# The Fourier transform of an attention block in plain float32: column tiles, a second feature fold, and a new written order

## The chip, the cores and the metric

The kernel runs on one core of a Trainium2 chip. The metric is device time in microseconds (us) of one launch, median of several runs. Engines are named as in the profile: PE (TensorE matmul), PEld (its weight loads), DVE (VectorE), ACT (ScalarE), POOL (GpSimd), SP (SyncE, which issues most DMAs).

## The reference

Softcapped attention over 4 batches, 12 heads, 448 tokens, head size 64; then a real two-dimensional Fourier transform over tokens and features, a layer norm and a feed-forward block:

```python
scores = cap * np.tanh(scale * (q @ k.T) / cap)
x = softmax(scores) @ v                # heads side by side: (4, 448, 768)
u = x + np.real(fft(fft(x, axis=1), axis=2))
un = (u - mean(u)) / sqrt(var(u) + 1e-6)
out = u + relu(un @ w_ch1) @ w_ch2     # 768 -> 3072 -> 768
```

The weights come as float64 values and are converted on the chip.

## The kernel before, in words

Nearly every large matmul is made of three float32r products: an operand is split into a head (a cast to float32r) and a rest (value minus head), and rest times head, head times rest and head times head are summed in PSUM. The weighing of v by the attention weights is the exception: it is in plain float32, and its 114 query rows are written as two column tiles of the array, output partitions 0 to 63 and 64 to 113.

*Attention.* Twelve heads of a batch make six pairs. Each pair has seven units of 128 keys; two units at a time go through `scores` (PE, line 428), `tanh` and `exp` (ACT, lines 438 and 441) and `weigh` (PE, line 459). `denominators` and `normalise` (DVE) write the batch's `u`.

*Transform of one batch.* A real transform needs only sums and differences of mirrored tokens and features. The queries are gathered so that the 448 tokens lie in four groups: odd, even, and the mirrors of both. `fold_tokens` adds and subtracts mirrored tokens; `fold_features` does so for a feature d and d + 384, so that 384 features are left, in three pieces of 128. There are two sorts, `sd` 0 and 1, for even and odd feature frequencies. `fold_split` and `fold_rest` split the result. `stage1` (line 527) is the transform over tokens: per piece and sort 12 matmuls of 226 columns with the constants `seqT`. `split_y` and `rest_y` split its result out of PSUM. `stage2` (line 551) is the transform over features: for cosine and sine (`n`) and odd and even tokens (`par`), 18 matmuls of 192 or 194 columns with the constants `featT`, themselves split by `constant`. `add_u`, `moments`, `rows`, `standardise`, `u_cols` and `u_copy` add it to u, standardise, and turn u around.

*Feed-forward.* `up` (line 761) and `down` (line 790) walk 12 groups of two blocks of 128 hidden features, over four batches, 36 matmuls of 448 columns each time; `first`, `second` and `third` convert the weights beside them on DVE and ACT.

*Order.* Each engine runs its instructions in program order. That order is written out: the table `ORDER` gives each call a place (`at`), calls are sorted by place and issued. From the second group of the feed-forward on, a fixed pattern takes over. Buffers are named by tag and count in `new`; PSUM results of `stage1`, `stage2`, `u_cols`, `rows_cols` and half of `down` share the tag `d` with two buffers, and scores have two buffers of their own.

Of the kernel before, what the change touches and what calls it, by code (L numbers as in the profile page):

```python
# [11 lines left out]
F32 = mybir.dt.float32  # L12
# [21 lines left out]
ODD = list(range(1, S // 2, 2))  # L34
EVEN = [0, S // 2] + list(range(2, S // 2, 2))
# [15 lines left out]
NJE, NJO = DM // 4 + 2, DM // 4  # L51
NJ = NJE + NJO
# [25 lines left out]
    [("y", 6)] * 6,  # L78
    [("qkr", 3)] * 3 + ["x1"] * 3,
    [("feat", 6)] * 6,  # L80
)
XCPLACE = [[(f"xc{b}", 3)] * 3 for b in range(3)] + [[("f", 2), ("f", 2), ("t", 1)]]
# [5 lines left out]
        313, 314, 296, 298, 539, 541, 592, 593, 786, 789, 794, 795, 987, 994, 988, 993  # L88
    ],
    "constant": [  # L90
        87, 36, 217, 35, 172, 14, 288, 12
    ],
    "denominators": [
        60, 84, 114, 153, 190, 227, 266, 323, 353, 397, 422, 469, 526, 560, 598, 634, 665, 714, 774, 814, 841,
        884, 920, 950
    ],
    "exp": [
# [4 lines left out]
    ],  # L102
    "fetch": [
        9, 62, 140, 155, 193, 203, 306, 307, 514, 636, 996, 1013, 1016, 1059
    ],
    "fold_features": [
        127, 92, 201, 169, 239, 255, 352, 368, 409, 421, 485, 488, 585, 588, 667, 649, 726, 722, 824, 822, 911,
        903, 960, 963
    ],
    "fold_rest": [  # L110
        152, 119, 222, 181, 264, 278, 385, 417, 455, 438, 505, 500, 631, 632, 698, 663, 751, 733, 864, 839, 933,
        929, 964, 968
    ],
    "fold_split": [
        128, 109, 218, 180, 257, 265, 359, 415, 452, 435, 504, 499, 587, 591, 697, 660, 740, 732, 863, 835, 914,
        906, 962, 966
    ],
    "fold_tokens": [
        89, 90, 162, 166, 236, 238, 343, 344, 404, 405, 483, 484, 573, 574, 640, 648, 718, 719, 817, 820, 894,
        898, 956, 957  # L120
# [5 lines left out]
        79, 26, 194, 28, 165, 13, 270, 7  # L126
    ],
    "load_qk": [
        1, 22, 41, 48, 93, 111, 176, 160, 233, 244, 338, 360, 349, 425, 482, 451, 501, 568, 638, 659, 720, 712,
        797, 724  # L130
    ],
    "load_v": [
        20, 43, 97, 129, 151, 167, 208, 253, 322, 361, 398, 433, 474, 497, 538, 575, 600, 679, 681, 777, 825,
        851, 861, 877
    ],
    "moments": [
        319, 336, 328, 334, 544, 555, 626, 613, 790, 793, 801, 808, 995, 997, 1005, 1002
    ],
    "normalise": [
        61, 66, 85, 88, 123, 122, 161, 157, 191, 192, 229, 234, 269, 272, 324, 325, 355, 354, 402, 399, 426,  # L140
        424, 475, 470, 535, 536, 572, 571, 603, 599, 639, 635, 671, 669, 717, 715, 780, 775, 816, 815, 845, 843,
        887, 885, 925, 921, 952, 951
    ],
    "operand": [
        564, 597, 946, 943, 984, 971, 1011, 1012, 1019, 1008, 1004, 1000, 1063, 1027, 978, 1068, 1069, 1071,
        1086, 1073, 1056, 1092, 1070, 1083
    ],
    "operand_rest": [
        739, 623, 953, 944, 985, 975, 1015, 1014, 1020, 1009, 1017, 1022, 1065, 1048, 1023, 1076, 1077, 1072,
        1093, 1080, 1081, 1112, 1091, 1089  # L150
    ],
    "product": [
# [3 lines left out]
    ],  # L156
    "residual": [
        977, 992, 983, 1010, 1025, 1024, 1051, 1053, 1066, 1079, 1036, 1050, 1078, 1108, 1075, 1106, 1119, 1116,
        1130, 1111, 1105, 1139, 1138, 1117
    ],  # L160
    "rest_k": [
        6, 29, 56, 75, 133, 136, 198, 235, 292, 308, 346, 365, 432, 458, 531, 523, 594, 629, 687, 711, 762, 787,
        830, 870
    ],
    "rest_q": [
        8, 31, 45, 82, 137, 149, 197, 212, 251, 315, 358, 390, 423, 441, 496, 520, 576, 608, 689, 692, 754, 771,
        850, 881
    ],
    "rest_y": [
        211, 144, 267, 262, 281, 287, 400, 437, 494, 472, 521, 529, 647, 682, 736, 695, 766, 756, 891, 860, 961,  # L170
        965, 974, 981
    ],
    "row": [
        976, 1021, 1074, 1104
    ],
    "rows": [
        374, 641, 809, 1026
    ],
    "rows_cols": [
        383, 642, 862, 1033  # L180
    ],
    "rows_copy": [
        389, 643, 868, 1034
    ],
    "rows_out": [
        445, 446, 583, 589, 686, 745, 785, 806, 869, 889, 901, 912, 1084, 1085, 1087, 1094
# [829 lines left out]
```

## Time and profile before

| | |
|---|---|
| median of 3 runs | 973.59 us (972.98 to 973.75) |
| profiled execution, own time | 975.0 us |
| its span, first to last instruction | 972.7 us |
| granted TensorE clock, mean | 0.998 |
| busy PE / PEld / DVE / ACT | 955.1 / 861.6 / 752.8 / 383.6 us |
| weighing of v, plain float32 (line 459) | 98.6 us busy |
| scores (line 428) | 79.3 us |
| transform over tokens (line 527) | 36.7 us |
| transform over features (line 551) | 30.7 us |
| feed-forward (lines 761 and 790) | 357.8 and 362.2 us |

The busy time of a group is the union of its instructions, and a matmul's record lasts from its start until its last result is out. So the mean length of one record is much longer than the time from one start to the next, and the times of PE groups that follow each other overlap a little. Throughput is read from starts. A plain float32 matmul leaves two records, a float32r one or a transposition leaves one: line 459 issues 1344 matmuls and has 2688 records, line 639 issues 96 transpositions and has 96.

### The profile page before, as it was taken

The page shows a single profiled execution, that of the slowest core. Times are in us where ns is not written, and L with a number is a line of the kernel's source. Part 1 is how long each engine was busy: PE and PEld are TensorE (multiplying, and loading weights), DVE is VectorE, ACT ScalarE, POOL GpSimd, SP SyncE. Part 2 cuts the span into 40 slices and gives each one's busy share as a digit, 9 for nine tenths or more (in the row PEclk, how much of TensorE's full clock was granted, in tenths as well). Part 3 has the DMA queues.
Part 4 walks back from the last instruction along what each step waited for, and adds up shares of the span by engine and source line. Part 5 has one row for each costly group of instructions (what it writes and reads, how often), then busy time and mean ns, then how long its engine had stood idle before and what let it go on. Part 6 is the DMA issues. An engine that isn't in the chain of part 4 may idle for free.

```text
span 972.7 us, 17798 instructions
## 1 busy us (share of the span) xinstructions
PE 955.1 (98%) x7328; PEld 861.6 (89%) x7328; DVE 752.8 (77%) x1510; ACT 383.6 (39%) x603; POOL 18.4 (2%) x50
## 2 busy tenths in 40 slices
PE   5999999999999999999999999999999999999998
PEld 4888898888888999999999998999999999999997
DVE  4799688695998878787787877877787787877733
ACT  6998999979461212212212122221222222122100
POOL 0001001020010000000000000000000000000000
PEclk9999999999999999999999999999999999999999
DMA  6443333311200221121121112111111211211123
GB/s 202 136 128 124 100 83 96 87 47 27 84 11 10 65 66 59 50 63 61 50 66 58 59 50 63 52 50 53 61 50 53 62 50 51 63 50 50 33 105 123
DMA packets 51376, 66.81 MB, mean 69 GB/s; under 512 B 30816, under 2 KB 35936, under 8 KB 51296
## 3 DMA queue, kind: packets, MB, share of 16 engines
q1 hardware_dynamic: 51216, 65.44, 22.6%
q8 instruction: 57, 0.93, 0.4%
q10 hardware_dynamic: 80, 0.25, 0.1%
q14 instruction: 23, 0.19, 0.1%
HBM read 60.16 MB, written 5.52 MB: 68 GB/s over the span
## 4 chain that ended last, share of the span: by engine, by line
PE 88%; ACT 6%; DVE 4%; DMA 1%; issue 1%; POOL 1%; SPq 0%; ACTq 0%; DVEq 0%
PE po L790 36%; PE ph L761 35%; PE av L459 6%; PE s L428 5%; PE yps L527 2%; PE pq L551 2%; ACT a L441 2%; ACT a L438 2%; ACT u L630 1%; PE pt L639 1%; DVE u L576 1%; DMA capt<-cap 1%; DMA dev<-lnrow 0%; DVE bs L585 0%; ACT khl L320 0%
## 5 line engine op out<-in xcount | busy, mean ns | idle before, releaser
L790 PE MATMUL po<-hh,w 128*128 128x448 f32 x1728 | 362.2, 367 | 1.1 <-DVE hh L773 0.6
L761 PE MATMUL ph<-xs,w 128*128 128x448 f32 x1728 | 357.8, 365 | 0.0
L790 PEld LDWEIGHTS po<-hh,w 128*128 128x128 f32 x1728 | 322.7, 188 | 33.7 <-DVE xc L799 3.0
L761 PEld LDWEIGHTS ph<-xs,w 128*128 128x128 f32 x1728 | 324.0, 188 | 26.5 <-issue 0.2
L799 DVE TENSOR_TENSOR xc<-xc,po 128x448 f32<-128x448 f32 x288 | 176.3, 617 | 42.8 <-PE po L790 42.1
L674 ACT ACTIVATE wt<-raw 128x384 f32<-128x384 f32 x96 | 53.6, 558 | 235.8 <-DVE w L706 235.4
L773 DVE SCALAR_TENSOR_TENSOR hh<-ph,hh 128x448 fp32r<-128x448 f32 x96 | 59.9, 624 | 96.8 <-ACT hh L772 96.6
L772 ACT ACTIVATE hh<-ph 128x448 fp32r<-128x448 f32 x96 | 52.3, 545 | 179.6 <-PE ph L761 179.6
L459 PEld LDWEIGHTS av<-vt,a 128*64 128x64 f32 (+1 forms) x2688 | 90.6, 131 | 14.3 <-issue 8.7
L459 PE MATMUL av<-vt,a 128*64 128x65 f32 (+3 forms) x2688 | 98.6, 230 | 2.1 <-PE s L428 0.8
L320 ACT CAST w<-wt 128x384 fp32r<-128x384 f32 x96 | 49.2, 512 | 123.5 <-DVE wt L681 123.4
L438 ACT ACTIVATE a<-s,tscale 128x904 f32<-128x904 f32 x84 | 84.6, 1024 | 10.7 <-PE s L428 8.4
L428 PE MATMUL s<-qhl,khl 64*128 64x452 f32 (+1 forms) x504 | 79.3, 402 | 9.6 <-DVE khl L325 8.5
L441 ACT ACTIVATE a<-a,capt 128x904 f32<-128x904 f32 x84 | 86.7, 1062 | 0.4
L428 PEld LDWEIGHTS s<-qhl,khl 64*128 64x128 f32 (+1 forms) x504 | 51.1, 192 | 22.4 <-DVE khl L325 8.5
L681 DVE SCALAR_TENSOR_TENSOR wt<-wt 128x384 f32<-128x384 f32 x96 | 53.6, 558 | 14.2 <-ACT wt L674 4.7
L678 DVE SCALAR_TENSOR_TENSOR wt<-raw,wt 128x384 uint32<-128x384 uint32 x96 | 53.6, 558 | 3.3
L700 DVE SCALAR_TENSOR_TENSOR wt<-raw,wt 128x384 f32<-128x384 uint32 x96 | 53.6, 558 | 3.3
L706 DVE TENSOR_TENSOR w<-wt 128x384 fp32r<-128x384 f32 x96 | 53.6, 558 | 3.4
L325 DVE TENSOR_TENSOR wt<-wt,w 128x384 f32<-128x384 f32 x96 | 52.8, 550 | 1.6 <-ACT w L320 1.6
L527 PEld LDWEIGHTS yps<-seqT,f 113*128 113x128 f32 (+1 forms) x288 | 33.8, 191 | 4.3 <-issue 1.5
L527 PE MATMUL yps<-seqT,f 113*128 113x226 f32 (+1 forms) x288 | 36.7, 279 | 0.7 <-DVE f L325 0.5
(66 smaller groups left out, 493.7 us busy)
## 6 DMA issues: line engine op xcount, KB each, us to landing
raw<-w2r SPq DMA_DIRECT2D x48, 384.0 KB
raw<-w1r SPq DMA_DIRECT2D x48, 384.0 KB
qkr<-qkT SPq DMA_DIRECT2D x23, 482.0 KB
vt<-vr SPq DMA_DIRECT2D x24, 288.0 KB
outT<-xc SPq DMA_DIRECT2D x24, 224.0 KB
fraw<-feat SPq DMA_DIRECT2D x6, 193.0 KB
dev<-lnrow SPq DMA_DIRECT2D x4, 224.0 KB
mean<-lnrow SPq DMA_DIRECT2D x4, 224.0 KB
```

The lines of the kernel that those rows point to most:

```text
L428: nc.tensor.matmul(ps_t[t][:, i, :SQ], khl[p % 2][rows, ik, k0 : k0 + P], qhl[p % 2][rows, iq], start=(k_ == 0), stop=(k_ == 2),)
L438: nc.scalar.activation(a_t[t], ps_t.pop(t)[:, :, :SQ], AF.Tanh, scale=tscale)
L441: nc.scalar.activation(a_t[t], a_t[t], AF.Exp, scale=capt)
L459: nc.tensor.matmul(pa_t[p][q0:q1, g // 2, o : o + n_ * (D + 1)], a_t[t][:, n, OFF[g] + q0 : OFF[g] + q1], v, start=u % 7 == 0 and g % 2 == ...
L527: nc.tensor.matmul(ps[:, n * NT2 : (n + 1) * NT2], f[:cnt, ia, 2 * n + c], seqT[n][:cnt, ib, c], start=(k_ == 0), stop=(k_ == 5),)
L674: nc.scalar.activation(w, hi, AF.Abs)
L678: nc.vector.scalar_tensor_tensor(tu, hi.bitcast(U32), 0xC0000000, tu, op0=ALU.bitwise_and, op1=ALU.bitwise_or)
L681: nc.vector.scalar_tensor_tensor(t, w, HI_MIN, t, op0=ALU.is_ge, op1=mul)
L761: nc.tensor.matmul(ph[:, :S], w_[:, dc * P : (dc + 1) * P], x_, start=(k_ == 0), stop=(k_ == 3 * NDC - 1),)
L773: nc.vector.scalar_tensor_tensor(hh[:, 1], ph[:, :S], 0.0, f32(hh[:, 0]), op0=ALU.max, op1=sub)
L790: nc.tensor.matmul(po[:, :S], w_[:, dc * P : (dc + 1) * P], hh[:, x_], start=(k_ == 0), stop=(k_ == 3 * GF - 1),)
L799: nc.vector.tensor_tensor(ac, ac, po[:, :S], op=add)
```

## The change

The transform no longer splits its operands: `constant`, `fold_split`, `fold_rest`, `split_y` and `rest_y` are gone, and `stage1` and `stage2` are plain float32 in two column tiles each. `fold_tokens` writes all of a batch into one tile, `mirror` folds feature d with 768 - d, and `fold_features` folds d with 384 - d, which leaves 193 sums, in two pieces of 97 and 96. `stage1` computes, per piece and sort, four products of 113 columns (cosine and sine, from odd and from even tokens); `combine` copies the one half out of PSUM on ACT and adds and subtracts it to the other on DVE, which gives frequency m and 224 - m. `ODD` and `EVEN` list the tokens in those pairs. `stage2` sums over two pieces instead of three. Some tiles get other tags, and exp has five buffers instead of four. `ORDER` is a new table; two of its lines stand in the diff.

```diff
+H2 = S // 2
+KODD, KEVEN = list(range(1, H2 // 2, 2)), list(range(0, H2 // 2 + 1, 2))
+ODD = [k for m in KODD for k in (m, H2 - m)]
+NF = DM // 4 + 1
+FW = (NF // 2 + 1, NF // 2)
+NK = len(KODD + KEVEN)
...
 ORDER = {
     "product": [
-        967, 969, 989, 998, 999, 1001, 1003, 1006, 1007, 1018, 1028, 1031, 1032, 1038, 1039, 1040, 1041, 1049,
+        857, 875, 892, 897, 898, 903, 911, 912, 913, 926, 927, 928, 932, 936, 937, 938, 947, 959, 969, 974, 975,
...
     def load_constant(i):
-        n, p = divmod(i, 4)
-        if p < 3:
-            raw = featT[n, p] = new([P, NJ], F32, "ff", 2, "fraw")
-            nc.sync.dma_start(raw, feat[n, :, p])
+        n, p = divmod(i, 2)
+        if p == 0:
+            featT[n] = new([P, 2, S], F32, "feat", 2, "featT")
+            nc.sync.dma_start(featT[n][:, :, :NJ], feat[n])
         else:
-            raw = seqT[n] = new([P, 2, NT2], F32, "ff", 2, "sraw")
-            nc.sync.dma_start(raw, seq[n])
+            seqT[n] = new([P, 2, NK], F32, "seq", 2, "seqT")
+            nc.sync.dma_start(seqT[n], seq[n])
...
+    def mirror(b, n):
+        t = t_t[b][:R, n]
+        nc.vector.tensor_tensor(t[:, :, 1 : DM // 2], t[:, :, 1 : DM // 2], t[:, :, : DM // 2 : -1], op=(add, sub)[n])
+
+    def fold_features(b, sd, n):
...
+        nc.vector.tensor_tensor(
+            f_t[b, sd][:R, 2 * n : 2 * n + 2],
+            t[:, :, :NF],
+            t[:, :, DM // 2 : DM // 4 - 1 : -1],
+            op=(add, sub)[sd != n],
+        )
...
     def stage1(b, p, sd):
+        f, p0, w = f_t[b, sd], p * FW[0], FW[p]
         ps = d_t["y", b, p, sd] = psum.tile([P, 512], F32, tag="d", name="yps")
         for n in range(2):
-            k_ = 0
             for c in range(2):
-                cnt = CNT[c]
-                for ia, ib in ((1, 0), (0, 1), (0, 0)):
+                o = (2 * n + (c == n)) * NK
+                for q0, q1 in ((0, D), (D, w)):
                     nc.tensor.matmul(
-                        ps[:, n * NT2 : (n + 1) * NT2],
-                        f[:cnt, ia, 2 * n + c],
-                        seqT[n][:cnt, ib, c],
-                        start=(k_ == 0),
-                        stop=(k_ == 5),
+                        ps[q0:q1, o : o + NK],
+                        f[: CNT[c], 2 * n + c, p0 + q0 : p0 + q1],
+                        seqT[n][: CNT[c], c],
+                        start=True,
+                        stop=True,
                     )
...
+    def combine(b, p, sd):
...
+        half = new([P, 2, NK], F32, "yh", 2, "yh")[:w]
+        copy("combine", b, half, ps[:, :, 1])
+        for k_, op in enumerate((add, sub)):
...
+            nc.vector.tensor_tensor(out, ps[:, :, 0], half, op=op)
...
         for sd, (j0, nj) in enumerate(SDJ):
-            k_ = 0
-            for p in range(3):
-                for iy, im in ((1, 0), (0, 1), (0, 0)):
+            for p, w in enumerate(FW):
+                for q0, q1 in ((0, D), (D, R)):
                     nc.tensor.matmul(
-                        ps[:R, j0 : j0 + nj],
-                        y_t[b, p, sd][:, iy, k0 : k0 + R],
-                        featT[n, p][:, im, j0 : j0 + nj],
+                        ps[q0:q1, j0 : j0 + nj],
+                        y_t[b, p][:w, sd, k0 + q0 : k0 + q1],
+                        featT[n][:w, p, j0 : j0 + nj],
```

Three places of the new order. First, PE at the first `stage1` of the program before (in a row: line, operation, output and operands with their buffer numbers, partitions x columns of the output, count).

```order
L428 MATMUL s_502<-qhl_82,khl_79 128x452 x6
L527 MATMUL yps_511<-seqT_195,f_476 128x226 x6
L527 MATMUL yps_511<-seqT_122,f_476 128x226 x6
L459 MATMUL av_537<-vt_80,a_410 64x130
L459 MATMUL av_537<-vt_80,a_410 50x130
```

And PE at the second `stage1` of the changed program, which is of the piece with 96 sums.

```order
L436 MATMUL av_815<-vt_80,a_844 50x130
L506 MATMUL yps_934<-seqT_646,ff_847 64x113
L506 MATMUL yps_934<-seqT_646,ff_847 32x113
...
L506 MATMUL yps_934<-seqT_787,ff_847 64x113
L506 MATMUL yps_934<-seqT_787,ff_847 32x113
...
L405 MATMUL s_943<-qhl_82,khl_79 128x452 x6
```

Twelve full-width matmuls become eight, alternately 64 and 32 columns of the array wide (each pair stands twice in the order, for odd and for even tokens); the other piece alternates 64 and 33.

Second, PE behind the last weighing of v, where the last batch is transformed: before,

```order
L527 MATMUL yps<-seqT,f 128x226 x24
L761 MATMUL ph<-xs,w_1014 128x448 x12
L527 MATMUL yps<-seqT,f 128x226 x24
L551 MATMUL pq<-featT,y 114x194 x9
L551 MATMUL pq<-featT,y 114x192 x9
```

and now, where the eight matmuls of each of the four `stage1` follow in one run:

```order
L436 MATMUL av<-vt,a 50x65
L747 MATMUL ph<-xs,w_1120 128x448 x6
L621 MATMUL pt<-ident,u 128x113
L621 MATMUL pt<-ident,u 128x112
...
L747 MATMUL ph<-xs,w_1120 128x448 x6
...
L506 MATMUL yps<-seqT,ff 64x113
L506 MATMUL yps<-seqT,ff 32x113
```

Four of the last batch's six `stage1` stood at this place, two of them right behind the weighing; now all four of the last batch stand behind 12 feed-forward matmuls and 12 transpositions.

Third, DVE at the same place, from the last `denominators` on: before,

```order
L475 RECIPROCAL den<-den 114x8
L481 TENSOR_TENSOR u<-av,den 114x2x128 x2
L325 TENSOR_TENSOR xs<-xc,xs 128x448
L500 TENSOR_TENSOR tf<-u 114x512 x2
L506 TENSOR_TENSOR ff<-tf 114x512
```

and now:

```order
L452 RECIPROCAL den<-den 114x8
L458 TENSOR_TENSOR u<-av,den 114x2x128 x2
L477 TENSOR_TENSOR tf<-u 114x4x128 x2
L483 TENSOR_TENSOR tf<-tf 114x2x383
L491 TENSOR_TENSOR ff<-tf 114x386
L483 TENSOR_TENSOR tf<-tf 114x2x383
L491 TENSOR_TENSOR ff<-tf 114x386
L315 TENSOR_TENSOR xs<-xc,xs 128x448
L491 TENSOR_TENSOR ff<-tf 114x386 x2
L526 TENSOR_TENSOR y<-yps,yh 96x2x113 x2
```

The folds over features now come once for the whole batch, behind its last pair of heads.

## Rows read from the trace of the kernel before

**Rows 1.** The page, busy time of each engine with its share.
```profile
PE 955.1 (98%) x7328; PEld 861.6 (89%) x7328; DVE 752.8 (77%) x1510; ACT 383.6 (39%) x603; POOL 18.4 (2%) x50
```
**Rows 2.** Busy us by stretch: its length, engines (instructions), clock, DMA share, GB/s.
```profile
10.00:244.00 234.00, 230.49 (x3722) 198.29 (x3718) 184.68 (x400) 220.65 (x289) 13.36 (x30) 0.99 0.35 98
244.00:265.00 21.00, 20.14 (x157) 18.89 (x154) 20.12 (x39) 7.47 (x15) 0.00 (x0) 1.00 0.28 98
265.00:972.70 707.70, 702.94 (x3451) 643.27 (x3449) 544.82 (x1062) 151.88 (x293) 4.07 (x10) 1.00 0.18 56
```
**Rows 3.** Waits of PE: who, for whom, us in total, times, longest.
```profile
PE s L428 <- DVE khl L325: 8.5, 1, 8.5
```
**Rows 4.** Timeline of PE: start us, us until the last end, instruction, records.
```profile
47.74 1.50 PE L527 MATMUL yps<-seqT,f 112*128 112x226 f32 x12
49.17 1.15 PE L459 MATMUL av<-vt,a 128*64 128x65 f32 x32
50.25 1.50 PE L428 MATMUL s<-qhl,khl 64*128 64x452 f32 x12
```
**Rows 5.** Timeline of PE around the first transform over features.
```profile
76.45 3.80 PE L551 MATMUL pq<-featT,y 128*114 128x194 f32 x36
80.18 1.09 PE L428 MATMUL s<-qhl,khl 64*128 64x452 f32 x8
```
**Rows 6.** Timeline of PE around weighings of 130 columns.
```profile
97.82 1.15 PE L459 MATMUL av<-vt,a 128*64 128x130 f32 x16 [0.59 <-PE s L428]
98.90 1.50 PE L428 MATMUL s<-qhl,khl 64*128 64x452 f32 x12
```
**Rows 7.** Chain that ended last: start us, us until the next piece, what.
```profile
180.76 2.01 PE av L459 x63
```
**Rows 8.** Timeline of PE around a transposition of eight columns.
```profile
223.33 0.36 PE L608 MATMUL rt<-ident,ln 114*8 114x114 f32 x2
223.62 0.56 PE L459 MATMUL av<-vt,a 128*64 128x65 f32 x12
```
**Rows 9.** Groups by line and form: count, busy us, mean ns, idle us before.
```profile
L608 PE MATMUL rt<-ident,ln 114*8 114x114 f32 x8 | 1.4, 263 | 0.0
L459 PE MATMUL av<-vt,a 128*64 128x65 f32 x1152 | 75.8, 223 | 1.4 <-issue 0.7 <-ACT a L441 0.5 <-PE s L428 0.2
L459 PEld LDWEIGHTS av<-vt,a 128*64 128x64 f32 x1344 | 90.6, 137 | 14.3 <-issue 8.7 <-ACT a L441 2.1 <-PE s L428 0.9
L325 DVE TENSOR_TENSOR f<-ff,f 114x512 fp32r<-114x512 f32 x24 | 16.4, 686 | 10.2 <-ACT f L320 10.2
L325 DVE TENSOR_TENSOR y<-yps,y 128x452 fp32r<-128x452 f32 x24 | 14.9, 620 | 8.2 <-ACT y L320 8.2
L506 DVE TENSOR_TENSOR ff<-tf 114x512 f32<-114x512 f32 x24 | 16.0, 685 | 0.3
L576 DVE TENSOR_TENSOR u<-u,pq 114x384 f32<-114x384 f32 x32 | 15.4, 544 | 0.0
L572 DVE TENSOR_TENSOR u<-u,pq 114x768 f32<-114x768 f32 x16 | 14.4, 946 | 0.0
L614 DVE COPY rowt<-rt 8x114 f32<-8x114 f32 x4 | 1.1, 263 | 4.4 <-PE rt L608 4.4
L320 ACT CAST f<-ff 114x512 fp32r<-114x512 f32 x24 | 15.2, 636 | 0.8 <-DVE ff L506 0.8
L320 ACT CAST y<-yps 128x452 fp32r<-128x452 f32 x24 | 13.1, 545 | 4.1 <-PE yps L527 4.0
```
**Rows 10.** Timeline of PE behind the last weighing of v.
```profile
244.30 2.95 PE L527 MATMUL yps<-seqT,f 112*128 112x226 f32 x24 [0.20 <-ACT xc L320]
247.08 2.61 PE L761 MATMUL ph<-xs,w 128*128 128x448 f32 x12
249.99 2.91 PE L527 MATMUL yps<-seqT,f 112*128 112x226 f32 x24 [0.30 <-DVE f L325]
254.97 2.34 PE L551 MATMUL pq<-featT,y 128*114 128x192 f32 x21 [0.37 <-DVE y L325]
```

More of the change, by code (lines that the diff above doesn't have):

```diff
@@ L28 @@
 KC = S // NKC
-ODD = list(range(1, S // 2, 2))
-EVEN = [0, S // 2] + list(range(2, S // 2, 2))
+H2 = S // 2
+KODD, KEVEN = list(range(1, H2 // 2, 2)), list(range(0, H2 // 2 + 1, 2))
+ODD = [k for m in KODD for k in (m, H2 - m)]
+EVEN = [k for m in KEVEN for k in (m, H2 - m)][:-1]
 ROWS = [ODD, EVEN, [S - k for k in ODD], [(S - k) % S for k in EVEN]]
@@ L247 @@
+        1041, 1042
     ],
@@ L259 @@
     "operand": "AAAA",
+    "combine": "AAAA",
     "weights_head": "A",
@@ L436, in tanh @@
     def tanh(t):
-        a_t[t] = new([P, 2, SQ], F32, "a", 4, "a")
+        a_t[t] = new([P, 2, SQ], F32, "a", 5, "a")
         nc.scalar.activation(a_t[t], ps_t.pop(t)[:, :, :SQ], AF.Tanh, scale=tscale)
@@ L508, in fold_split @@
-    def fold_split(b, p, sd):
-        f = f_t[b, p, sd]
-        t = f_t[b, p, sd] = new([P, 2, 4, P], F32R, "f", 2, "f"), f
-        copy("fold_split", b, t[0][:R, 0], f[:R])
-    def fold_rest(b, p, sd):
-        t, f = f_t[b, p, sd]
-        minus(t[:R, 1], f[:R], f32(t[:R, 0]))
-        f_t[b, p, sd] = t
+        if b not in t_t:
+            t_t[b] = new([P, 2, 2, DM], F32, "t", 1, "tf")
+        x, t = (z.rearrange("q g (e c) -> q g e c", e=2)[:, :, :, p * P : (p + 1) * P] for z in (u_t[b][:R], t_t[b][:R, pm]))
@@ new lines, in fold_tokens @@
+        nc.vector.tensor_tensor(t, x[:, :2], x[:, 2:], op=(add, sub)[pm])
+    def mirror(b, n):
+        t = t_t[b][:R, n]
+        nc.vector.tensor_tensor(t[:, :, 1 : DM // 2], t[:, :, 1 : DM // 2], t[:, :, : DM // 2 : -1], op=(add, sub)[n])
+    def fold_features(b, sd, n):
+        if (b, sd) not in f_t:
+            f_t[b, sd] = new([P, 4, NF], F32, "ff", 2, "ff")
+        t = t_t[b][:R, n]
+        nc.vector.tensor_tensor(
[4 more added lines that the diff above has]
+        )
@@ new lines, in stage1 @@
+                        stop=True,
+                    )
+    def combine(b, p, sd):
+        if (b, p) not in y_t:
+            y_t[b, p] = new([P, 2, 2 * NT2], F32, "y", 2, "y")
+        y, w = y_t[b, p][: FW[p], sd], FW[p]
+        ps = d_t.pop(("y", b, p, sd))[:w, : 4 * NK].rearrange("w (n e m) -> w n e m", n=2, e=2)
+        half = new([P, 2, NK], F32, "yh", 2, "yh")[:w]
+        copy("combine", b, half, ps[:, :, 1])
+        for k_, op in enumerate((add, sub)):
+            step = NT2 + (1, -1)[k_]
+            out = bass.AP(y.tensor, y.offset + k_, [list(y.ap[0]), [step, 2], [2, NK]])
+            nc.vector.tensor_tensor(out, ps[:, :, 0], half, op=op)
@@ L641, in u_cols, with place @@
             )
+    trio, used = {}, {}
+    def place(shape, dtype, where, name):
+        if type(where) is tuple:
+            return new(shape, dtype, *where, name)
+        if where not in trio:
+            trio[where] = new([P, 3, 2, S], dtype, where, 1, name)
+        used[where] = used.get(where, -1) + 1
+        return trio[where][:, used[where]]
     def u_copy(b, p):
         if (b, p // 2) not in xc:
-            xc[b, p // 2] = new([P, 2, S], F32, *XCPLACE[b][p // 2], "xc")
+            xc[b, p // 2] = place([P, 2, S], F32, XCPLACE[b][p // 2], "xc")
         copy("u_copy", b, xc[b, p // 2][:, p % 2], d_t.pop(("u", b, p))[:, :S])
@@ L727, in operand @@
     def operand(b, dc):
-        place = XPLACE[b][dc]
-        if place == "x1":
-            if dc == 3:
-                xs["x1"] = new([P, 3, 2, S], F32R, "x1", 1, "xs")
-            t = xs["x1"][:, dc - 3]
-        else:
-            t = new([P, 2, S], F32R, *place, "xs")
+        t = place([P, 2, S], F32R, XPLACE[b][dc], "xs")
         copy("operand", b, t[:, 0], xc[b, dc // 2][:, dc % 2])
@@ L770, in up @@
                     yield
-            hh = hs[b, n] = new([P, 2, S], F32R, "a", 4, "hh")
+            hh = hs[b, n] = new([P, 2, S], F32R, "a", 5, "hh")
             nc.scalar.activation(hh[:, 0], ph[:, :S], AF.Relu)
@@ L844, in attention_fft_ffn @@
     at(scales, needs=[("load_cap",)])
-    for i in range(8):
+    for i in range(4):
         at(load_constant, i)
-        at(constant, i, needs=[("load_constant", i)])
     convert(0, 8)
```

195 lines of the change are left out of this document (75 added, 120 removed), and 44 rows, old and new, of the table ORDER.

## The prediction, made before the changed kernel had run

> **What bounds the kernel now.** I read the busy times first, then the stretches, the waits of PE, and only then single rows of the timeline, because the shares say which engine to count on and the timeline gives the price of one step. PE is busy 98% of the span [rows 1]. In the stretch with attention and the first three transforms (10 to 244 us) PE is busy 230.5 of 234.0 us, and ACT 220.7 [rows 2]: PE sets the pace, and ACT is 10 us behind it. Behind that, from 265 us on, PE is busy 702.9 of 707.7 us and ACT is at a fifth, so the feed-forward is a row of matmuls. The one long wait of PE is 8.5 us for the first keys [rows 3]; it lies at the start, and the change does not touch it. So what the change takes from PE comes off the time, as long as ACT and the folds on DVE keep up; what it takes from DVE and ACT only keeps them off the path.
>
> **What goes and what comes on PE.** Stage 1 before: a set of 12 begins at 47.74 and the next work at 49.17, 1.43 us [rows 4]. 0.09 of it is a change of column setting (below), so a matmul takes 1.34 / 12 = 0.112 us. 24 sets of 12: 32.2 us. Stage 2 before: 36 matmuls from 76.45 to 80.18, 3.73 us, less 0.09, 0.101 us each [rows 5]; 16 sets of 18: 29.1 us. Together 61.3 us.
>
> The price of plain float32 in two column tiles is shown by the weighing of v. 64 records take 2.01 us [rows 7] and 32 take 49.17 to 50.25, 1.08 us [rows 4]. The difference, 0.93 us, is 32 more records, 16 in each tile: 0.058 us from one to the next in a tile, while a record itself lasts 0.223 [rows 9]; the two tiles run side by side. What is fixed in a group is 1.08 - 0.93 = 0.15 us, a change of setting and the first load of weights. 16 records of 130 columns also take 1.08 us (97.82 to 98.90) [rows 6], so twice the columns are twice the step: 0.058 / 65 = 0.9 ns a column in each tile.
>
> Stage 2 after: 8 matmuls a set, 16 records, 8 in each tile, 193 columns on average: 8 x 0.172 = 1.38 us. 16 sets: 22.0 us, 7.1 less than before. The tiles are 64 and 50 wide as in the weighing, so I carry it over; the shorter sums (97 and 96 partitions in place of 128) cost neither more nor less if the step is a matter of columns, as these rows say.
>
> Stage 1 after, the piece of 97 sums, tiles of 64 and 33: 8 x 0.101 = 0.81 us. Eight sets: 6.5 us.
>
> Stage 1 after, the piece of 96 sums, tiles of 64 and 32: here is the doubt. The nearest thing in the trace is the transposition of eight columns, `rt`. Its two records start 0.36 - 0.263 = 0.10 us apart [rows 8, 9], and the weighing, in tiles of 64, starts 0.29 us after the first: 0.09 us more than two steps. So from a narrow setting to the 64-wide one PE loses 0.09 us, and nothing runs side by side across it. If 32 columns are a setting of their own, as eight are here, the piece of 96 changes it at every one of its eight matmuls: its 16 records run in single file, 16 x 0.101 = 1.62 us, and eight changes cost between 0.09 (the change) and 0.15 (with the load of the first weights, the fixed part above) each. I take 0.12: 2.6 us a set. The bounds: 0.81 us if it behaves like the piece of 97, and 16 x 0.39 = 6.2 us if each record waits for its own load of weights, 0.137 us, and for all of the one before, 0.223 and 48 further columns [rows 9]. I take 2.6 because `rt` is the one row in which the width of a column tile changes. Eight sets: 20.8 us, so stage 1 is 27.3 against 32.2.
>
> The Trainium skill has a rule that speaks against this part of the change: "TensorEngine Tiling (Array Packing)", Key Properties, says that tiles work independently but that a change of the tiling mode drains TensorE, and its list of configurations has 128x64 and 128x32 apart. The row of `rt` agrees with it, at 0.09 us. By the rule a set of the piece of 96 costs the 2.6 us taken here; by the other sentence alone, that tiles run in parallel, 0.81.
>
> Beside the sets, the changes of setting themselves. Counted in the two orders, PE changes between full width, row halves for the scores and column tiles 136 times before and 120 times now, apart from those inside the piece of 96 (weighing, stage 1 and stage 2 now share a setting). 16 fewer, at 0.15 each: 2.4 us.
>
> Sum on PE: 61.3 - 22.0 - 27.3 + 2.4 = 14.4 us less.
>
> **DVE and ACT.** Gone on DVE: the rests of the folds, 16.4, and of stage 1, 14.9, the old fold, 16.0, and eight rests of constants [rows 9]. New: 8 mirrors of 766 elements (as the 768 of line 572, read backwards too, 0.946), 7.6; 16 folds of 386 (0.544), 8.7; 32 sums in `combine` of 226 (between 0.263 for 114 and 0.544 for 384: 0.38), 12.2. So 28.5 for 47.3 and more. Gone on ACT: 15.2 and 13.1 and the heads of the constants; new: 16 copies of 226 elements, between nothing and the 0.545 of a copy of 452, I take 0.33: 5.3. About 23 us less on ACT, some three quarters of it in the attention stretch. Neither gain counts by itself. They are what lets PE have its own: ACT would be at about 203 us there and PE at 220, further apart than now.
>
> **Where an edit costs.** Before, the last batch was folded piece by piece, and four of its six sets of stage 1 stood behind the last weighing: two directly, two behind 12 feed-forward matmuls, with waits of 0.20, 0.30 and 0.37 us [rows 10]. Now the folds over features come once, behind the last `normalise`: DVE has there two token folds (2 x 0.68), two mirrors (2 x 0.95) and two folds (2 x 0.54) to do before the first stage 1, 4.3 us and some 0.8 for the denominators and `normalise`. PE has in front of it 12 feed-forward matmuls, which took 2.61 us until their last end [rows 10], and 12 transpositions of 113 columns, which I put at 0.1 us each as `rt`'s records of 114: about 3.6 us. I put 1.5 us of new waiting on PE there; 0 is one end, and the other is the whole chain of 5 us with nothing in front. Behind it stand the four `combine`; their 2 x 0.38 and a copy are another 0.5 us until stage 2 can begin, in place of the 0.37 before. Elsewhere `stage1`, `combine` and `stage2` stand between weighings and scores, which cover the waits. The loads of the constants are fewer; nothing waited for them.
>
> Sum: 14.4 less on PE, 1.5 more waiting: 13 to 14 us. The profiled execution has a span of 972.7 and takes 975.0 as a whole; 975.0 - 13.5 = 961.5, and since that execution stands 1.4 above the median of the runs, 960 us in their terms. I forecast 959, since some small waits of PE on splits, as those in [rows 10], go with the splits.
>
> **The rivals.**
> 1. *The likeliest*: as above, 959 us, with 953 to 965 from the price of a change (0.09 to 0.15) and of the new wait. Chance 0.55.
> 2. *Widths of 64 and 32 share a setting*: the piece of 96 costs 0.81 us a set like that of 97. 8 x 1.8 = 14 us less again: 945 us. For it: both widths are cut from the same array, and the first tile is the same; against it: `rt`. ACT at 203 us would still be under PE at 210 in the attention stretch, but close, so 944 to 950. Chance 0.24.
> 3. *The gain is lost in waits of the new order*: ACT was busy 220.7 of 234 us [rows 2], and a scores, tanh, exp, weigh round has only two PSUM buffers. Where a batch's transform stands bunched on PE (all of it now follows the batch's last pair), ACT runs dry and later cannot make it up. The price is at most PE's gain in that stretch, some 10 us: 966 to 973. Chance 0.12. Against it: ACT and DVE lose as much work as PE.
> 4. *Slower*: in the piece of 96 every record waits for its own weights and for the end of the one before, 6.2 us a set instead of 2.6: 8 x 3.6 = 29 us, 988 us. It turns the sign from 2.6 + 14 / 8 = 4.3 us a set on, that is 0.27 us a record. Against it: at `rt` the change itself cost only 0.09, and second records of a matmul need no change. Chance 0.09.
>
> A measurement of this kernel tells about 0.2%, 2 us, from no change. Faster: 0.55 + 0.24 and most of the third case, 0.88; within 0.2%, the rest of the third: 0.03; slower: 0.09. The range for 8 in 10 takes in the second case and the upper part of the first: 943 to 967.
>
> **What would show it.** In the changed profile, a set of the piece of 97 should take some 0.9 us from its start to the next work and one of the piece of 96 some 2.6; if both take 0.9, rival 2 holds, and above 4.3 rival 4. A set of stage 2 should take 1.4 to 1.5 us. PE should stay above 97% busy, with a new wait of 1 to 2 us before the last batch's first stage 1. ACT's share of the attention stretch should be lower than PE's; if PE's idle time in that stretch is over 8 us, with releasers `a` or `s`, rival 3 holds. The forecast is wrong if the feed-forward, which does the same matmuls, does not take the same time.

## The result and the profile after

The changed kernel takes 955.87 us, median of 4 runs (955.11 to 956.33), against 973.38 us before; the ratio is 0.982, 95% interval 0.980 to 0.984. That is 17.5 us faster, inside the predicted range, 3.1 us below the forecast of 959. The profiled execution took 956.3 us with a span of 954.1.

The busy times of the page after, which answer to [rows 1], and the stretches, which answer to [rows 2] (length, PE, PEld, DVE, ACT and POOL busy, clock, DMA share, GB/s):

```profile
PE 939.2 (98%) x7264; PEld 834.5 (87%) x7264; DVE 733.6 (77%) x1486; ACT 362.3 (38%) x563; POOL 16.5 (2%) x50
```
```profile
10.00:226.00 216.00, 214.83 (x3649) 175.81 (x3646) 170.37 (x384) 204.31 (x258) 11.62 (x30) 1.00 0.37 105
226.00:247.00 21.00, 20.33 (x170) 15.14 (x171) 17.58 (x37) 4.96 (x12) 0.00 (x0) 1.00 0.01 2
247.00:954.10 707.10, 701.66 (x3440) 641.64 (x3438) 541.85 (x1055) 149.69 (x289) 3.85 (x10) 1.00 0.19 58
```

The attention stretch is 18 us shorter, 216 for 234, and PE is still 99% busy in it. The feed-forward is as long as it was, 707.1 us for 707.7. PE remains the engine that sets the pace, and it has less to do.

Where it went can be read from the starts of PE's records. I put the time from each record's start to the next one's to the first of the two, which counts waits in, and add by group ("all else" holds the transpositions and what runs after PE's last record starts):

| group of PE, us | before | after | two pieces of 97 (below) |
|---|---|---|---|
| stage 1 | 34.9 | 27.9 | 18.1 |
| stage 2 | 30.4 | 22.3 | 21.8 |
| scores | 78.1 | 75.1 | 75.6 |
| weighing of v | 96.5 | 94.8 | 96.5 |
| feed-forward | 708.5 | 710.0 | 710.0 |
| in front of the first score | 8.5 | 7.6 | 8.0 |
| all else | 15.9 | 16.3 | 16.3 |
| span | 972.7 | 954.1 | 946.2 |

The timeline of PE at the first two sets of stage 1 answers to [rows 4], in the same columns, and that of the first stage 2 to [rows 5]:

```profile
61.70 0.99 PE L506 MATMUL yps<-seqT,ff 112*64 112x113 f32 x16
62.51 2.02 PE L436 MATMUL av<-vt,a 128*50 128x65 f32 x48
64.36 2.61 PE L506 MATMUL yps<-seqT,ff 112*64 112x113 f32 x16
66.91 0.89 PE L405 MATMUL s<-qhl,khl 64*128 64x452 f32 x6
...
82.30 2.84 PE L534 MATMUL pq<-featT,y 97*64 97x194 f32 x32
84.97 0.63 PE L436 MATMUL av<-vt,a 128*50 128x65 f32 x16
```

The first set, of the piece of 97, runs from 61.70 to 62.51: 0.81 us. The second, of the piece of 96, from 64.36 to 66.91: 2.55 us for the same number of records with the same 113 columns. The only difference in the program is that its second tile is 32 columns wide instead of 33. The single records of the trace show how the time goes. In the first set they start in pairs, one in each tile, 6 to 19 ns apart. In the second none start together: the two records of a matmul start 0.10 to 0.15 us apart, and the first of the other width 0.19 us behind the last of the one before. Two sets of stage 2 take 82.30 to 84.97, 1.34 us each.

PE behind the last weighing, which answers to [rows 10]:

```profile
225.61 3.66 PE L506 MATMUL yps<-seqT,ff 112*64 112x113 f32 x32 [0.19 <-DVE ff L491]
229.71 3.59 PE L506 MATMUL yps<-seqT,ff 112*64 112x113 f32 x32 [0.45 <-ACT yh L310]
233.23 1.20 PE L534 MATMUL pq<-featT,y 97*64 97x194 f32 x12
234.63 1.85 PE L534 MATMUL pq<-featT,y 96*64 96x192 f32 x20 [0.20 <-DVE y L526]
```

Its waits are 0.19, 0.45 and 0.20 us, 0.84 together; before they were 0.20, 0.30 and 0.37. What DVE does in front of them, from the last `denominators` on:

```profile
221.42 0.23 DVE L451 TENSOR_SCALAR den<-av,guard 114x8 f32<-114x8 f32 x1 [0.46 <-PE av L436]
...
223.91 0.95 DVE L483 TENSOR_TENSOR tf<-tf 114x766 f32<-114x766 f32 x1
224.90 0.56 DVE L491 TENSOR_TENSOR ff<-tf 114x386 f32<-114x386 f32 x1
225.38 0.95 DVE L483 TENSOR_TENSOR tf<-tf 114x766 f32<-114x766 f32 x1
226.36 0.56 DVE L491 TENSOR_TENSOR ff<-tf 114x386 f32<-114x386 f32 x1
```

The first `stage1` starts at 225.61, as soon as the first of the two folds has ended.

### The profile page after: what moved, and what is told of

It is laid out like the page before. It is cut to its first block, busy times and chain, and to the rows that moved or that the text cites. A ratio compares the mean times of both kernels' runs of the same rounds, so it can differ in the third digit from the quotient of the medians.

```text
span 954.1 us, 17612 instructions
## 1 busy us (share of the span) xinstructions
PE 939.2 (98%) x7264; PEld 834.5 (87%) x7264; DVE 733.6 (77%) x1486; ACT 362.3 (38%) x563; POOL 16.5 (2%) x50
## 4 chain that ended last, share of the span: by engine, by line
PE 95%; DVE 2%; ACT 1%; DMA 1%; issue 1%; SPq 0%; DVEq 0%
PE ph L747 37%; PE po L776 36%; PE av L436 9%; PE s L405 7%; PE yps L506 3%; PE pq L534 2%; PE pt L621 1%; DMA qkr<-qkT 1%; ACT a L415 1%; ACT a L418 0%; DVE xc L737 0%; DVE xc L785 0%; ACT hh L758 0%; DVE hh L759 0%; DVE bs L567 0%
## 5 line engine op out<-in xcount | busy, mean ns | idle before, releaser
L759 DVE SCALAR_TENSOR_TENSOR hh<-ph,hh 128x448 fp32r<-128x448 f32 x96 | 60.0, 625 | 96.7 <-ACT hh L758 96.5
L436 PEld LDWEIGHTS av<-vt,a 128*50 128x50 f32 (+1 forms) x2688 | 91.4, 131 | 12.4 <-issue 9.1
L405 PE MATMUL s<-qhl,khl 64*128 64x452 f32 (+1 forms) x504 | 78.1, 400 | 8.2 <-DVE khl L315 7.6
L667 DVE TENSOR_SCALAR wt<-raw 128x384 uint32<-128x384 uint32 x96 | 34.2, 356 | 1.3
L689 DVE TENSOR_SCALAR wt<-wt 128x384 uint32<-128x384 uint32 x96 | 34.0, 354 | 0.4
```

The source lines that it names most:

```text
L405: nc.tensor.matmul(ps_t[t][:, i, :SQ], khl[p % 2][rows, ik, k0 : k0 + P], qhl[p % 2][rows, iq], start=(k_ == 0), stop=(k_ == 2),)
L436: nc.tensor.matmul(pa_t[p][q0:q1, g // 2, o : o + n_ * (D + 1)], a_t[t][:, n, OFF[g] + q0 : OFF[g] + q1], v, start=u % 7 == 0 and g % 2 == ...
L759: nc.vector.scalar_tensor_tensor(hh[:, 1], ph[:, :S], 0.0, f32(hh[:, 0]), op0=ALU.max, op1=sub)
```

## The experiments

Twelve kernels ran, each in three rounds against the kernel before. "Two pieces of 97" is the changed kernel with the first edit, and several later edits stand on it.

| kernel | us | ratio to before, 95% interval |
|---|---|---|
| changed kernel | 955.9 | 0.982 (0.980 to 0.984) |
| two pieces of 97 | 948.6 | 0.975 (0.973 to 0.976) |
| grouped by width | 951.3 | 0.977 (0.975 to 0.979) |
| full width | 949.7 | 0.976 (0.974 to 0.977) |
| folds and copies repeated | 991.9 | 1.019 (1.017 to 1.021) |
| folds repeated | 974.1 | 1.000 (0.999 to 1.001) |
| load beside the transform | 964.6 | 0.991 (0.989 to 0.992) |
| 97, standardise on DVE | 956.6 | 0.983 (0.981 to 0.984) |
| 97, q's head on ACT | 962.2 | 0.989 (0.987 to 0.990) |
| 97, q's rest on POOL | 952.4 | 0.979 (0.977 to 0.980) |
| 97, block moved forward | 950.4 | 0.977 (0.975 to 0.979) |
| 97, mirror cut short | 946.6 | 0.973 (0.971 to 0.974) |
| 97, standardise cut short | 948.9 | 0.975 (0.974 to 0.977) |

**1. Two pieces of 97: take the narrow tile away.**

```diff
-FW = (NF // 2 + 1, NF // 2)
+FW = (NF // 2 + 1, NF // 2 + 1)
...
-            d = (p * FW[0] + np.arange(w))[:, None]
-            half = np.where(d == NF - 1, 0.5, 1.0)
+            d = (p * (FW[0] - 1) + np.arange(w))[:, None]
+            half = np.where(d == NF - 1, 0.5, 1.0) * np.where((p == 1) & (d == FW[0] - 1), 0.0, 1.0)
...
-        f, p0, w = f_t[b, sd], p * FW[0], FW[p]
+        f, p0, w = f_t[b, sd], p * (FW[0] - 1), FW[p]
```

> Both pieces of the 193 sums get 97 partitions: the second begins at sum 96 instead of 97, its doubled first sum has weight 0 in the constants, so no matmul is 32 columns wide. Theory (a change between tiles of 64 and 32 columns stops PE, and PE sets the time): a set of the second piece falls from 2.59 to about 0.83 us, eight sets, 14 us; 942 us. Rival (ACT is so close behind PE in the attention stretch that it takes over): 947 to 951 us, with new waits of PE on ACT. Rival (the long sets are long for another reason, their buffer or their operands): 955 to 956 us, sets unchanged.

948.57 us: 7.3 us less, half of the 14. The mechanism is there: the second set of stage 1 now takes 62.75 to 63.66, 0.91 us. The time is only partly there, because PE now waits where it did not:

```profile
62.75 0.99 PE L506 MATMUL yps<-seqT,ff 112*33 112x113 f32 x16
63.66 0.88 PE L405 MATMUL s<-qhl,khl 64*128 64x452 f32 x6
...
111.93 0.99 PE L506 MATMUL yps<-seqT,ff 112*64 112x113 f32 x16
113.27 0.88 PE L405 MATMUL s<-qhl,khl 64*128 64x452 f32 x6 [0.35 <-ACT a L415]
...
219.72 0.58 PE L506 MATMUL yps<-seqT,ff 112*64 112x113 f32 x8 [0.19 <-DVE ff L491]
221.09 1.39 PE L506 MATMUL yps<-seqT,ff 112*64 112x113 f32 x24 [0.79 <-DVE ff L491]
223.40 1.76 PE L506 MATMUL yps<-seqT,ff 112*64 112x113 f32 x32 [0.92 <-DVE y L526]
225.81 2.82 PE L534 MATMUL pq<-featT,y 97*64 97x194 f32 x32 [0.65 <-DVE y L526]
```

The sets in front of a score are as long as before the score's PSUM buffer is free (113.27, waiting for `tanh`), and behind the last weighing the waits are 0.19 + 0.79 + 0.92 + 0.65 = 2.55 us where they were 0.84. So a part of the slow sets had been waiting time in another form: while PE worked through 2.6 us, DVE finished the next fold. Eight sets at 0.81 to 0.91 us instead of 2.55 are some 13 to 14 us less, and all waits of PE together are 5.7 us longer than in the changed kernel, which leaves about the 7.9 us by which the span fell. The rival that ACT is close behind had named 947 to 951 us and holds in the number; the row at 221.09 shows that folds and sums on DVE are in it too.

**2. Grouped by width: fewer changes, nothing more side by side.** In the piece of 96 the loop over tiles is outside, so four matmuls of 64 come before four of 32.

```diff
-        for n in range(2):
-            for c in range(2):
-                for q0, q1 in ((0, D), (D, w)):
+        for q0, q1 in ((0, D), (D, w)):
+            for n in range(2):
+                for c in range(2):
```

> In the piece of 96 the four matmuls of 64 columns are issued first and then the four of 32, so that a set changes its setting once inside instead of seven times; nothing runs side by side in it still. Theory: 16 records at 0.10 and two changes, about 1.8 us a set instead of 2.59, 6 us over eight sets; 949 to 950 us. Rival (the price of a set is that the two widths do not run side by side, the change itself is free): 16 x 0.16 either way, 955 to 956 us.

951.28 us, 1.3 above the theory's 949 to 950. The set takes 64.25 to 66.02, 1.77 us, as expected of 16 records in single file with one change:

```profile
64.25 1.84 PE L519 MATMUL yps<-seqT,ff 112*64 112x113 f32 x16
66.02 1.31 PE L405 MATMUL s<-qhl,khl 64*128 64x452 f32 x10
```

Against 2.55 us, six changes fewer save 0.78: 0.13 us for a change, in the predicted 0.09 to 0.15. What is left above 0.9 us, another 0.9, is that the records do not run side by side. In this run that has a second reason, since matmuls of the same tile now stand behind each other; that tiles of 64 and 32 do not overlap even when they alternate is shown by the starts of the single records in the changed kernel.

**3. Full width: no column tiles at all.**

```diff
-                for q0, q1 in ((0, D), (D, w)):
+                for q0, q1 in ((0, w),):
...
-                for q0, q1 in ((0, D), (D, R)):
+                for q0, q1 in ((0, R),):
```

> Stage 1 and stage 2 as plain float32 at the full width of the array, one matmul where two column tiles stood, half as many records. Theory (a record costs its columns, and 97 or 114 output partitions fit the array at once, so tiles that only cut one matmul in two give nothing): a set of stage 1 is 8 x 0.10 = 0.8 us for both pieces, a set of stage 2 stays at 1.4 us, and some 20 more changes of setting against the weighing cost 3 to 4 us; 944 to 947 us. Rival (two tiles side by side are what makes plain float32 pay; one wide load of weights sets the step at 0.19 us): a set of stage 1 1.5 us, 952 to 960 us.

949.70 us, between the theory's 944 to 947 and the rival's 952 to 960, and two pieces of 97 do not beat it by more than their intervals. Eight records of a set go by in 59.64 to 60.59, 0.95 us, and it makes no difference whether the piece has 97 sums or 96:

```profile
59.64 1.02 PE L506 MATMUL yps<-seqT,ff 112*97 112x113 f32 x8
60.59 2.05 PE L436 MATMUL av<-vt,a 128*64 128x65 f32 x48
62.57 1.02 PE L506 MATMUL yps<-seqT,ff 112*96 112x113 f32 x8
63.52 0.68 PE L405 MATMUL s<-qhl,khl 64*128 64x452 f32 x4
```

So the gain of the change did not come from the column tiles. It came from fewer and shorter matmuls in plain float32: one wide record of 113 columns costs about what two tiles side by side cost, and the tiles as written cost 6 us more. How much of the gain is the format and how much the new folds was not told apart: the new folds with three float32r products did not run.

**4. and 5. Work given back to DVE and ACT inside the transform.** Both repeat the fold over features; the first repeats the copy of `combine` as well.

```diff
+        for i in range(3):
             nc.vector.tensor_tensor(
                 f_t[b, sd][:R, 2 * n : 2 * n + 2],
...
+        for i in range(5):
             copy("combine", b, half, ps[:, :, 1])
```

> The changed kernel with about the work given back to ACT and DVE that the change took from them: each copy of combine is made five times (22 us more on ACT in all) and each fold over features three times (17 us more on DVE). Theory (the change pays through PE alone, but it needs ACT under PE): ACT, 204 of 216 us in the attention stretch, would be at some 220 and set the pace there; 960 to 965 us. Rival (ACT and DVE had room enough): 956 to 957 us. Rival (most of the gain came from the relief of ACT and DVE): 968 us and more.

> The changed kernel with each fold over features made three times (17 us more on DVE), the copies of combine once: one half of the load run. Theory (ACT was what that run lacked): DVE has 8 us of 50 to spare, 957 to 960 us. Rival (the delay of the folds in front of stage 1 was half of the 36 us): 968 to 975 us.

991.86 us with both, 974.11 us with the folds alone. Both are far above what I expected of an engine with room to spare; the rivals that named 968 us and more, and 968 to 975 us, hold in the number. With the folds alone, 17 us of work on an engine that is busy 77% cost 18 us, which is the whole gain of the change. The rows show why, on an execution of 971.4 us whose span is 15.0 us longer than the changed kernel's. PE in that run, around the second batch's stage 1, and busy times in four short stretches there:

```profile
117.84 0.88 PE L405 MATMUL s<-qhl,khl 64*128 64x452 f32 x6
120.83 3.84 PE L507 MATMUL yps<-seqT,ff 112*64 112x113 f32 x14 [2.11 <-DVE ff L492]
```
```profile
114.00:118.00 4.00, 4.00 (x55) 3.48 (x54) 3.86 (x7) 4.00 (x8) 0.00 (x0) 1.00 0.90 271
118.00:120.80 2.80, 0.72 (x6) 0.33 (x7) 2.73 (x6) 2.80 (x4) 0.00 (x0) 1.00 0.65 253
120.80:124.10 3.30, 3.27 (x13) 1.46 (x14) 3.09 (x7) 0.25 (x2) 0.00 (x0) 0.51 0.00 0
124.10:130.00 5.90, 5.90 (x31) 3.45 (x32) 4.97 (x11) 3.15 (x5) 0.00 (x0) 0.70 0.28 70
```

Stage 1 stands in PE's order in front of the next scores. When the folds are late, PE waits 2.11 us, and then its granted clock is 0.51, the lower level of 1.2 GHz, for 3.3 us and 0.70 on average for the 5.9 us behind it. So the wait is paid once as such and a second time in clock: (1 - 0.51) x 3.3 + (1 - 0.70) x 5.9 = 3.4 us. The clock falls in two more places of that run, each time behind waits of over 1 us:

```profile
69.66:73.07 3.41, 3.41 (x33) 2.81 (x33) 3.27 (x9) 0.72 (x2) 0.00 (x0) 0.50 0.39 114
240.32:247.15 6.83, 5.07 (x40) 3.55 (x37) 4.40 (x11) 1.43 (x4) 0.00 (x0) 0.50 0.00 0
```
```profile
PE yps L507 <- DVE ff L492: 6.3, 5, 2.1
PE yps L507 <- DVE y L528: 1.8, 1, 1.8
```

Together that is 17.1 us at 0.50, or 8.5 us of lost clock, beside 8.1 us of waits of stage 1 for folds and sums. All waits of PE are 9.8 us longer than in the changed kernel, so not all of the lost clock shows in the time. That the waits bring the clock down is read from their order and was not tested; a single wait of 2.1 us in run 10 was not followed by a fall. With the copies repeated too, the clock is at 0.50 for 34 us in all, and stage 2 and the transpositions wait for copies and sums as well.

**6. Load beside the transform.** Instead of the transform's chain, work that runs ahead is repeated.

```diff
+        for i in range(2):
             minus(qhl[p % 2][:, 1], qk[p][:, :SQ], f32(qhl[p % 2][:, 0]))
...
+        for i in range(2):
             copy("k", p // NP, khl[p % 2][:, 0], qk[p][:, SQ:])
```

> The changed kernel with more load on ACT and DVE, but outside the transform: the head of k is cast twice (15 us more on ACT in all) and the rest of q is computed twice (15 us more on DVE). Theory (it is the amount of work: ACT is 204 of 216 us busy there): ACT goes to the limit, 962 us and more. Rival (it is the chain inside the transform, stage 1 to copy to sums to stage 2, that must not get longer; in the run with copies and folds repeated it did): 956 to 960 us.

964.59 us, 8.7 more, for 15 us on each engine; the theory had named 962 us and more. ACT is 214.9 of 221 us busy in the stretch from 10 to 231 us:

```profile
10.00:231.00 221.00, 215.41 (x3641) 172.94 (x3640) 182.53 (x406) 214.88 (x275) 13.00 (x30) 1.00 0.36 103
```

The clock stays at 1.00 and the waits are many and short; the one that grew most is that of scores for `tanh`, 2.3 us where the changed kernel had 0.5. ACT has come up to PE. So both of the disputed reasons are real: load beside the chain cost about half of what was put on each engine, and in the chain, where a batch's folds come in one piece, about all of it. Both engines were loaded at once here; which of them cost the time was not told apart.

**7. to 9. Moving work between engines, on two pieces of 97.** `"standardise": "DDDA"` for `"AAAA"`; `"q": "AAAA"` for `"DDDD"`; and the rest of q on POOL:

```diff
-        minus(qhl[p % 2][:, 1], qk[p][:, :SQ], f32(qhl[p % 2][:, 0]))
+        (nc.gpsimd if p > 1 else nc.vector).tensor_tensor(
+            qhl[p % 2][:, 1], qk[p][:, :SQ], f32(qhl[p % 2][:, 0]), op=sub
+        )
```

> As the run with two pieces of 97, with standardise of the first three batches on DVE instead of ACT: 12 us less on ACT in the attention stretch, 8 to 11 us more on DVE. Theory (behind PE, ACT sets that stretch: it is 48 us busy of 50 there): most of what two pieces of 97 left behind comes out, 943 to 945 us. Rival (PE waits for the folds and sums on DVE, whichever engine standardises): 948 to 951 us.

> As the run with two pieces of 97, with the head of q cast on ACT instead of DVE: 9 us less on DVE, some 12 us more on ACT, which is 48 of 50 us busy there. The opposite of moving standardise to DVE, which cost 8 us. Theory (both engines are at PE's heels, and each piece of work sits where the written order has room for it): ACT becomes the pace, 954 to 962 us. Rival (only DVE was short): 944 to 947 us.

> As the run with two pieces of 97, with the rest of q computed on POOL instead of DVE from the third pair on: 22 x 0.62 = 14 us less on DVE, POOL otherwise idle. Theory (in that run PE waits for work that is queued on DVE): 2 to 5 us of the missing 7 come out, 944 to 947 us. Rival (POOL is slow and the scores wait for it, or it takes the memory port from DVE): 952 us and more. Rival (DVE's queue is not it): 948 to 949 us.

All three are slower than the 948.6 they start from: 956.63, 962.17 and 952.36 us. Work off ACT and onto DVE costs 8 us, work off DVE and onto ACT 14, and work off DVE onto a nearly idle POOL 4. In the first, the transpositions wait for the standardised rows 6.6 us; in the third, an instruction that takes DVE 0.63 us takes POOL 1.16 by its records, and two scores wait for it:

```profile
PE pt L621 <- DVE u L614: 6.6, 5, 3.0
```
```profile
PE s L407 <- POOL qhl L390: 2.0, 2, 1.7
```
```profile
L390 POOL TENSOR_TENSOR qhl<-qkr,qhl x22: 1136/1160/1536, 15.0 to 202.1; 128x452 fp32r<-128x452 f32 x22
L390 DVE TENSOR_TENSOR qhl<-qkr,qhl x2: 623/626/630, 7.8 to 10.8; 128x452 fp32r<-128x452 f32 x2
```

DVE pays for it too. It gave up 14 us of work in the third run and is only 5.5 us less busy than in two pieces of 97 (727.0 for 732.5 us). Some of its instructions, not all, get longer when POOL works beside them, as this one, which takes 0.56 us elsewhere:

```profile
79.77 1.41 DVE L694 SCALAR_TENSOR_TENSOR wt<-raw,wt 128x384 f32<-128x384 uint32 x1
```
```profile
79.55 1.21 POOL L390 TENSOR_TENSOR qhl<-qkr,qhl 128x452 fp32r<-128x452 f32 x1 [10.31 <-DVE qhl L312]
```

Of the theories only that of the second run held, 0.2 us above the upper end of its numbers: it says that each piece of work sits where the written order has room. The theories of the other two, that one engine is simply short, fell. In the first its rival (948 to 951 us) fell as well; in the third the rival of 952 us and more holds, with a slow POOL and a DVE that takes longer beside it.

**10. A block moved forward.** Only `"product"` changes: `881, 886, 892, 897` for `892, 897, 898, 903`.

> As the run with two pieces of 97, and four pieces of the first feed-forward block moved forward in the written order, between and behind the last batch's stage 1 (places 881, 886, 892, 897 for 892, 897, 898, 903). There the last four sets took 6.09 us for 3.3 us of work. Theory (the last batch's chain over DVE and ACT is bare since its matmuls got short): 2 to 3 us come out, 946 us. Rival (the wait only moves to the next link of the chain): 948 to 949 us.

950.44 us, not faster. The waits of 0.92 and 0.65 us behind the last weighing are gone, and others stand further on, where the moved matmuls are now missing:

```profile
PE po L776 <- DVE xc L785: 2.7, 3, 2.1
...
PE pt L621 <- ACT xc L310: 0.7, 1, 0.7
```

In two pieces of 97 the first of these is 1.4 us. The rival, that the wait moves to the next link, holds in kind, 1.4 us above its 949.

**11. and 12. Work left out, on two pieces of 97.**

```diff
-        nc.vector.tensor_tensor(t[:, :, 1 : DM // 2], t[:, :, 1 : DM // 2], t[:, :, : DM // 2 : -1], op=(add, sub)[n])
+        nc.vector.tensor_tensor(t[:, :, 1:9], t[:, :, 1:9], t[:, :, : DM - 9 : -1], op=(add, sub)[n])
```

```diff
-            nc.scalar.activation(u, u, AF.Identity, bias=bias, scale=scale)
+            nc.scalar.activation(u[:, :96], u[:, :96], AF.Identity, bias=bias, scale=scale)
```

> As the run with two pieces of 97, with only 8 of the 383 mirrored features added or subtracted, so the fold over mirrored features is left out for the rest: 6.4 us less on DVE, all of it in the chain in front of stage 1. Theory (that chain is what two pieces of 97 left bare): 943 to 945 us, and the waits of PE for folds gone. Rival (ACT is what is left): 948 to 949 us.

> As the run with two pieces of 97, with only 96 of the 768 features of each row standardised: some 11 us less on ACT, three quarters of it in the attention stretch, nothing more on DVE. Theory (ACT is at the limit there): 942 to 945 us. Rival (the folds on DVE are what is left): 947 to 949 us.

The first leaves out the mirror fold for all but 8 of 383 features, the second the standardising of all but 96 of 768. They take 946.64 and 948.91 us. With the short mirror the waits for the folds go and 1.9 us with them, between the theory (943 to 945 us) and the rival (948 to 949). With the short standardise ACT loses 6 us in the stretch and the time does not move, as its rival said:

```profile
10.00:219.00 209.00, 204.31 (x3645) 170.52 (x3642) 168.69 (x382) 202.32 (x256) 11.61 (x30) 1.00 0.38 109
```
```profile
10.00:219.00 209.00, 204.45 (x3648) 170.84 (x3644) 169.10 (x384) 196.55 (x256) 11.63 (x30) 1.00 0.38 109
```

(The first line is two pieces of 97, the second that with the short standardise.) So the 7 us that two pieces of 97 did not give are not a lack of ACT as a whole. 2 of them are the folds in front of stage 1. The others are spread over the waits of PE, which are 5.7 us longer in all than in the changed kernel, some 3.6 of it for DVE (folds, sums and the rests of keys) and 1.6 for ACT. The rows that grew most, in two pieces of 97, and then the first of them in the changed kernel, where the folds have 0.2 us in place of 1.0:

```profile
PE s L405 <- ACT a L415: 1.8, 4, 0.9
...
PE pq L534 <- DVE y L526: 1.1, 2, 0.7
PE yps L506 <- DVE ff L491: 1.0, 2, 0.8
PE yps L506 <- DVE y L526: 0.9, 1, 0.9
```
```profile
PE s L405 <- ACT a L415: 0.5, 1, 0.5
```

That the written order, which was made for longer sets, is what brings them is likely but not shown: a table written anew for these lengths was not tried.

## Why the prediction was right, and where it was not

*PE sets the time.* Right: the span fell by 18.6 us, and stage 1, stage 2, the scores and the weighing fell by 19.8 together, waits counted in. The sum had 14.4; 2.8 of the 19.8 are waits that got shorter.

*Stage 2, 7.1 us.* Right in kind, a little low: 8.1. After the change it is 22.3 us by starts where I had 22.0. The missing 1 us is on the side of before, 30.4 by starts against 29.1, for which I had left out a wait of 0.37 us and counted the changes of setting elsewhere.

*Stage 1.* Both prices were right: 0.81 us for the piece of 97, as forecast, and 2.55 for the piece of 96 for which I had taken 2.6 between 0.81 and 6.2. The one row about a narrow transposition pointed to the right case, but it has 8 columns, not 32: that 32 is a setting apart from 64 and that 33 is not is shown only now, by this profile and runs 1 to 3, with the change at 0.13 us and the lost overlap. The Trainium skill's rule that a change of the tiling mode drains TensorE ("TensorEngine Tiling (Array Packing)", Key Properties) agrees with this trace: 2.55 us against 0.81 where 32 columns stand for 33. Stage 1 as a whole gave 7.0 us for 4.9, again on the side of before: 34.9 us by starts, against 32.2 without the changes.

*16 fewer changes of setting, 2.4 us.* A little high. Scores and weighing together fell by 4.7 us. The waits directly behind them fell from 3.7 to 0.6 us, so 1.6 us are left for the changes there. The waits that went are the larger part; the forecast had about 1 us for them.

*The new wait, 1.5 us.* Wrong. "I put 1.5 us of new waiting on PE there": the wait in front of the first stage 1 is 0.19 us, and all of them at that place are 0.84 us against 0.87. I had set both mirrors and both folds in front of the first stage 1, 5.1 us with `denominators` and `normalise`. Its first matmuls read the first fold alone, which ends 4.0 us after `denominators` begins (221.42 to 225.46), and PE has 4.1 us of other matmuls and transpositions there (221.29 to 225.42). The second fold, until 226.92, is covered to about 0.1 us because the piece of 96 comes first and its first eight records last nearly until then. Run 1 shows the cover by taking it away: 0.79 us of waiting for that fold, 2.55 us of waits in all.

*The sum.* By spans the change gave 18.6 us where I had 13 to 14. The wait that did not come is 1.5 of the difference, other waits that got shorter are about 2, and the matmuls of the four groups with their changes of setting gave 17.0 us without waits for 14.4. Against that, the feed-forward is 1.5 us longer by starts. By the medians the forecast was 3.1 us high.

*"Neither gain counts by itself. They are what lets PE have its own", of DVE and ACT.* This holds, but it was priced for ACT alone (203 us under PE at 220), with DVE only named as a condition. Run 5 puts back on DVE about 17 of the 19 us that the change took from it (752.8 to 733.6 us), and the kernel is at 974.1 us, no faster than before; run 6, off the chain, loses half of the gain. So the room on DVE, 23% idle on average, was not room in front of stage 1. Run 5 puts the work in one piece in front of stage 1, which is not where all of it had been, so it does not show that the shorter matmuls alone would have gained nothing; that kernel was not tried.

*Rival 3, waits of the new order,* did not occur in the changed kernel (0.5 us of PE for `tanh`, 0.4 for the copies). In two pieces of 97 longer waits, more for DVE than for ACT, took 5.7 us of the gain.

A small slip in the working: 0.137, 0.223 and 48 columns at 0.9 ns add up to 0.40 us a record, not 0.39, so rival 4 stands at 6.4 us a set. The forecast does not change by it.

## What to carry to other kernels

Where two column tiles are to run side by side, look at the width of the narrower one: here one of 32 beside one of 64 ran in single file and paid for each change, and one of 33 did not; and where the output fits the array, first ask whether a single full-width matmul is not as fast. In a kernel whose order is written out, idle time on a second engine is not room: price an added instruction at its full length when it stands in the chain in front of the busy engine (here 17 us cost 18), and at a part of it elsewhere. A gain on the bounding engine came through only as far as the chain around it kept up: half of the 14 us of two pieces of 97.

## What the runs showed of the hardware that was not expected

One column of width decides: 16 records of 113 columns in tiles of 64 and 33 take 0.81 us, in tiles of 64 and 32 2.55 us. A set of stage 1 in plain float32 takes 0.95 us at full width and 0.81 to 0.91 in two tiles side by side: cutting 97 output partitions in two gained next to nothing. A wait of PE of 2.1 us, after a stretch at full clock, was followed by 3.3 us at a granted clock of 0.51, and in the whole run with folds repeated 8.5 us of clock were lost beside 8.1 us of waits of stage 1; another wait of 2.1 us, in run 10, brought no fall. An instruction of DVE that takes 0.56 us took 1.41 with a subtraction of POOL beside it.
